# V products of batch 0 in two steps, and a new order of all steps around them, in a fused attention and gMLP kernel

## The chip, the cores and the metric

The kernel runs on one core of one Trainium2 chip. The metric is device time in microseconds (us) of one execution; the given time is the median of three runs. TensorE is called PE, VectorE DVE, ScalarE ACT, GpSimd POOL; SP issues the transfers.

## What is computed

Sliding-window attention over 8 batches, 8 heads, 576 positions and head size 64 (a query sees itself and the 63 positions before it), then a gMLP block on its output. Cut to what matters:

```python
scores = scale * np.matmul(q, k.transpose(0, 1, 3, 2))
rel = pos[:, None] - pos[None, :]
scores = np.where((rel >= 0) & (rel < 64), scores, -1e9)
attn = softmax(scores)
x = np.matmul(attn, v)            # (8, 576, 512) with heads side by side
h = np.maximum(x @ w_in, 0.0)     # w_in: 512 x 1024
u, v = h[..., :512], h[..., 512:]
v_n = (v - mean(v)) / np.sqrt(var(v) + 1e-06)
v_s = np.einsum('ts,bsd->btd', w_spatial, v_n) + b_spatial[None, :, None]
out = (u * v_s) @ w_out           # float32
```

## The kernel before

The work is cut into some 1,100 named steps. Each names the engine that runs it, what it depends on and which buffers it takes. A list, ORDER, gives every step in the order of emission as `name:engine:buffer`. Each engine runs its own steps in that order, strictly one after the other, so the place of a step in the list sets what it waits behind. Where the engine is PH in place of PE, the step's matmuls of 128 output partitions are issued as two of 64 (`halves`, L588 to L593); steps with PE there issue them whole. The buffer number names a slot; a step that takes a slot waits until the last users of what was there are done.

In the names the first digit is the batch, and `_g` is a group of four heads, `_gu` a pair of heads (u is 0 or 1) of a group, r the last 64 positions.

- ldq, ldk, ldv: transfers on SP's queue (L404, L425), in slots "nat" (8) and "natv" (4). ldwin, ldwsp, ldwo and ldb bring the weights (L330, L346, L387, L355) through the same "nat" slots.
- cq, ck, cv: cast to 16 bits, on POOL (L299, L302, L304; q and k in three pieces), DVE (L304) or ACT (L296). sl, su, s4 shift v by 64 positions. cwin, cwsp, cwo cast weights, cb the bias row.
- tq, tk: transpose on DVE (L411). S: scores on PE (L471, L539 for r). E: exponential on ACT (L478, L549). M: mask by a minimum on DVE (L481, L553). Z: row sums on PE (L494, L562). N and n: logarithm and its negative exponential on ACT, the reciprocal (L521, L523). P: products with v on PE (L506, L575). X: the division on DVE, which writes one head pair of x (L514, L583).
- V: `x @ w_in[:, 512:]` for 128 positions, four accumulated products, one for each head pair r of x (L657 to L661). V_4 is for the last 64 positions and takes along the last 64 output rows of the batch before (L673, L676). Vr, Vb, Va: Relu on ACT (L640), statistics and aggregate on DVE (L642, L644). L1, L2: the inverse deviation on ACT (L687, L689). A: normalisation on DVE (L699).
- U and Ur: the other half of `x @ w_in`, and its Relu (L728). W and We: w_spatial transposed on PE (L371), and copied out. G: the spatial product over five A tiles (four and one with the bias row). Ge: its product with u on DVE (L758). O: the output product, Oe its copy (L617), st its transfer.
- D: 27 matmuls on zeros (L798) that keep PE busy while the first data is on its way: 25 of two 512-column products, D25 and D26 of nine 128-column ones.

W_k needs all five cwsp casts, G needs all A steps of its batch and all We. Before V0 can begin there must be x of batch 0 and the casts of the second half of w_in.

## Time and profile before

| | us |
|---|---|
| median of three runs | 199.06 (198.86 to 200.04) |
| the profiled execution | 197.47 |
| its span, first to last instruction | 195.7 |
| PE / DVE / ACT / POOL busy in it | 186.3 / 164.1 / 150.0 / 111.3 |
| granted PE clock, mean | 0.998 |

How the rows of the profile are read. A row of the timeline has start, duration, engine, line of the kernel, operation, output<-input, shapes, and the count of instructions merged; in brackets the idle time of the engine before it and what ended that. A row of waits has who waited for whom, the total, how often, and the longest. A row of a stretch has its length and then each engine's busy time with its count of instructions, in the order PE, PE's weight loads, DVE, ACT, POOL, then the granted clock, the share of time in which the 16 DMA engines were busy, and GB/s. Ends of matmuls are modelled: consecutive rows of PE overlap by up to 0.2 us, and the start of the next row tells more than the duration.

### The profile page before, as it was taken

Reading aid. Unit: us, or ns where it says so; the run is one execution under the profiler, and the core shown is the slowest. Engines: PE = TensorE matmul, PEld = TensorE weight load, DVE = VectorE, ACT = ScalarE, POOL = GpSimd, SP = SyncE. Lnnn points to the kernel's source line nnn. Section 1 sums busy time; section 2 is a strip of 40 time slices with the busy share of each in tenths; the row PEclk is TensorE's granted clock in tenths of the full one; section 3 lists DMA queues with packets and bytes.
Section 4 is the critical chain, followed back from the end, with each engine's and each line's share of the span. In section 5 each row is a group of like instructions: output and inputs, shape, how many; then the busy total and the mean of one; then the engine's idle time right before and its main releaser. Section 6 shows DMA issues by size and latency. Waiting matters only on the chain.

```text
span 195.7 us, 7663 instructions
## 1 busy us (share of the span) xinstructions
PE 186.3 (95%) x3230; PEld 106.8 (55%) x3230; DVE 164.1 (84%) x305; ACT 150.0 (77%) x281; POOL 111.3 (57%) x196
## 2 busy tenths in 40 slices
...
GB/s 210 378 302 183 364 372 225 297 343 384 241 246 301 352 170 275 315 208 300 289 258 220 290 166 180 280 134 51 293 132 155 66 0 113 150 0 2 180 116 191
DMA packets 50277, 42.73 MB, mean 218 GB/s; under 512 B 39361, under 2 KB 39489, under 8 KB 50242
## 3 DMA queue, kind: packets, MB, share of 16 engines
...
q8 instruction: 25, 0.41, 0.9%
q10 hardware_dynamic: 224, 0.33, 0.5%
...
## 4 chain that ended last, share of the span: by engine, by line
PE 61%; DVE 14%; DMA 8%; SPq 6%; POOL 5%; issue 2%; ACT 2%; POOLq 0%; DVEq 0%
PE bank L593 38%; PE bank L590 10%; SPq L425 5%; DMA nv<-in_v_dram 3%; PE pair L471 3%; DVE e L481 3%; PE bank L506 3%; DVE kT L411 3%; DMA wi<-in_moe_w_in_dram 3%; DMA nk<-in_k_dram 3%; PE bank L673 3%; DVE vn L699 2%; PE bank L494 2%; POOL hk L299 2%; DVE x L514 1%
## 5 line engine op out<-in xcount | busy, mean ns | idle before, releaser
L478 ACT ACTIVATE e<-pair 128x1024 f16<-128x1024 f32 x32 | 31.5, 1025 | 13.5 <-PE pair L471 13.0
L593 PE MATMUL bank<-wspT,vn 128*64 128x512 f16 (+3 forms) x490 | 35.6, 290 | 0.6 <-DVE vn L699 0.4
L299 POOL CAST hk<-nk 128x384 f16<-128x384 f32 x42 | 22.5, 569 | 17.7 <-DMA nk<-in_k_dram 9.6
L758 DVE TENSOR_TENSOR g<-bank,ru 128x512 f16<-128x512 f32 (+1 forms) x40 | 24.5, 625 | 7.5 <-PE bank L593 4.5
L642 DVE BATCH_NORM_STATS2 st<-vs 128x6 f32<-128x512 f16 (+1 forms) x40 | 26.1, 669 | 4.6 <-ACT vs L640 4.4
L640 ACT ACTIVATE vs<-bank 128x512 f16<-128x512 f32 (+1 forms) x40 | 23.2, 595 | 8.6 <-PE bank L593 6.3
L302 POOL COPY hs<-hv 64x512 f16<-64x512 f16 (+1 forms) x46 | 28.4, 644 | 1.2
L617 ACT COPY ob<-bank 128x512 f32<-128x512 f32 (+1 forms) x39 | 22.1, 589 | 8.4 <-PE bank L590 6.4
L593 PE MATMUL bank<-x,win 128*64 128x512 f16 (+1 forms) x328 | 27.6, 308 | 0.0
L593 PE MATMUL bank<-win,x 128*64 128x512 f16 x208 | 26.2, 380 | 0.2 <-DVE x L514 0.2
L481 DVE TENSOR_TENSOR e<-e,mask 128x1024 f16<-128x1024 f16 x32 | 25.1, 803 | 0.8 <-ACT e L478 0.7
L299 POOL CAST hq<-nq 128x384 f16<-128x384 f32 x39 | 21.3, 583 | 5.9 <-DMA nq<-in_q_dram 3.6
L593 PEld LDWEIGHTS <-vn 128*64 128x64 f16 (+1 forms) x490 | 18.1, 111 | 11.8 <-DVE vn L699 1.4
L728 ACT ACTIVATE ru<-bank 128x512 f32<-128x512 f32 (+1 forms) x40 | 21.6, 555 | 3.3 <-PE bank L593 3.1
L593 PE MATMUL bank<-wout,g 128*64 128x512 f16 x184 | 22.6, 379 | 0.0
L514 DVE TENSOR_TENSOR x<-bank,lz 128x512 f16<-128x512 f32 x32 | 21.0, 681 | 1.4 <-PE bank L506 1.2
L411 DVE STREAM_TRANSPOSE kT<-hk 128x576 f32<-128x576 f32 x16 | 19.9, 1243 | 1.2 <-POOL hk L299 1.2
L521 ACT ACTIVATE lz<-bank 128x512 f32<-128x512 f32 x32 | 18.8, 598 | 2.6 <-PE bank L494 2.5
L699 DVE TENSOR_SCALAR vn<-vs,mv,ln 128x512 f16<-128x512 f16 (+1 forms) x40 | 17.3, 482 | 3.9 <-ACT ln L689 3.9
L302 POOL CAST hv<-nv 128x512 f16<-128x512 f32 x24 | 17.1, 738 | 5.4 <-DMA nv<-in_v_dram 5.0
L523 ACT ACTIVATE lz<-lz 128x512 f32<-128x512 f32 x32 | 19.8, 636 | 0.3
L411 DVE STREAM_TRANSPOSE qT<-hq 128x576 f32<-128x576 f32 x16 | 19.8, 1240 | 0.1
...
## 6 DMA issues: line engine op xcount, KB each, us to landing
...
ws<-in_moe_w_spatial_dram SPq DMA_DIRECT2D x4, 288.0 KB, 6.7
...
```

The lines of the kernel that those rows point to most:

```text
L299: nc.gpsimd.tensor_copy(o[:, n:n + 384], i[:, n:n + 384])
L302: nc.gpsimd.tensor_copy(o[:, lo:hi, :, :], i[:, lo:hi, :, :])
L411: d = add(f"t{name}{b}_{g}", ("DVE", 1.09), key, lambda e: nc.vector.transpose(qt.t[:, :].rearrange("p (i j) -> p j i", j=18), h.t[:, :].b ...
L478: ex = add(f"E{b}_{g}{u}", ("ACT", 0.91), key, lambda e, u=u: nc.scalar.activation(e2[u].t[:, :, :], sc[u].t[:, :, :], AF.Exp, bias=0.0, s ...
L481: mins.append(add(f"M{b}_{g}{u}", ("DVE", 0.65), key, lambda e, u=u: nc.vector.tensor_tensor(e2[u].t[:, :, :], e2[u].t[:, :, :], mask[:, : ...
L514: lambda e, u=u, ob=ob, lz=lz: nc.vector.tensor_tensor(x.t[:, u, :], ob.t[:, :], lz.t[:, :], ALU.mult),
L593: nc.tensor.matmul(o[c:c + 64, :], w[:, c:c + 64], x, start=start, stop=stop)
L617: lambda e: (nc.vector.tensor_copy if last else nc.scalar.copy)(view(), m.t[rows, 0:n]),
L640: rl = add(f"Vr{b}_{j}", ("ACT", 0.49), key, lambda e: nc.scalar.activation(vs.t[0:jn, :], m.t[0:jn, :], AF.Relu), deps=[pv], acq=[vs], us ...
L642: s1 = add(f"Vb{b}_{j}", ("DVE", 0.6), key + 0.02, lambda e: nc.vector.bn_stats(st6.t[0:jn, 0:6], vs.t[0:jn, :]), deps=[rl], acq=[st6], us ...
L728: lambda e, m=m, ru=ru, n=n: nc.scalar.activation(ru.t[:, 0:n], m.t[:, 0:n], AF.Relu), deps=[pu], acq=[ru], uses=[m])))
L758: lambda e, m=m, g=g, ru=ru, n=n: nc.vector.tensor_tensor(g.t[:, 0:n], m.t[:, 0:n], ru.t[:, 0:n], ALU.mult),
```

## The change

Three things change.

1. The four V steps of batch 0 over 128 positions (V0_0 to V0_3) are cut in two. Y0_j makes the products of head pairs 0 and 1 (group 0), V0_j then those of pairs 2 and 3 (group 1) into the same bank. Y0_j depends on X0_00 and X0_01 and two of the w_in casts alone. Y0_2, Y0_3 and V0_3 run ahead of Z1_00, the others later.
2. ORDER is another list. The transfers keep their order but for ldwin101, which goes ahead of ldwin110 and ldwin111; some take other slots. 32 steps have another engine, 25 of them in the first third of the list: ck0_0 (DVE to POOL), ck0_1 (POOL to ACT), cq1_0 (DVE to ACT), cv0_10, cwin111 and cwin010 (DVE to POOL), cwin011 (ACT to POOL), cwin100 and cwsp2 (POOL to DVE), su0_10 and s40_1 (ACT to DVE), su0_00 and s40_0 (POOL to ACT), We0 and We2 (DVE to ACT), We4 (ACT to DVE), sl1_00 (DVE to POOL), su1_01, cv1_11, sl1_11 and cq2_0 (ACT to POOL), cv1_10, sl1_10, su1_10 and ck2_1 (POOL to ACT). After them cwo01 goes to ACT and cwo10 to POOL, s44_1, s45_0 and su6_00 from ACT to POOL, cv7_10 and sl7_10 from POOL to ACT.
3. 114 steps stand as PH where 109 did: 16 names are new among them (Y0_0 is one), 11 are gone.

No arithmetic is added or removed: the matmuls of Y0_j and V0_j together are those of V0_j before. The diff, with the list cut to its start (to S3_0, the first scores of batch 3) and its end (from V7_4):

```diff
-D10:PE:0 D23:PE:1 D20:PE:2 D24:PE:3 D4:PE:0 D13:PE:1 D5:PE:2 ldq0_0:DQ:0 cq0_0:DVE:0 D15:PE:3
-tq0_0:DVE:0 D6:PE:0 ldk0_0:DQ:1 ldk0_1:DQ:2 ck0_1:POOL:1 ldq0_1:DQ:3 ldv0_00:DQ:0 D3:PE:1
-ldq1_0:DQ:4 ck0_0:DVE:2 tk0_0:DVE:1 D16:PE:2 tk0_1:DVE:2 D26:PE:3 S0_0:PE:0:1 E0_00:ACT:0
-ldk1_0:DQ:5 ldv0_10:DQ:1 ldv0_11:DQ M0_00:DVE cq0_1:POOL:3 tq0_1:DVE:3 D14:PE:0 D17:PE:1 D19:PE:2
-E0_01:ACT:1 D21:PE:3 S0_1:PE:0:1 M0_01:DVE E0_10:ACT:2 E0_11:ACT:3 ldv0_01:DQ ldv0_02:DQ Z0_01:PE:0
-N0_01:ACT:0 D7:PE:1 cq1_0:DVE:0 ck1_0:POOL:2 D25:PE:2 tq1_0:DVE:4 cv0_10:DVE:0 sl0_10:POOL:0
-su0_10:ACT D0:PE:3 D1:PE:1 cv0_00:POOL:1 M0_10:DVE S0_r:PE:0:1 E0_r0:ACT:0 E0_r1:ACT Z0_00:PE:2
-ldv0_12:DQ ldv0_03:DQ ldwin100:DQ:6 ldv0_04:DQ M0_11:DVE tk1_0:DVE:5 sl0_00:POOL:1 su0_00:POOL
-M0_r:DVE Z0_10:PE:3 ldv0_13:DQ ldv0_14:DQ cv0_01:DVE Z0_11:PE:1 su0_01:DVE sl0_01:DVE cv0_11:DVE
-cwin100:POOL su0_11:DVE D11:PE:0 s40_0:POOL ldwin110:DQ:7 ldwin111:DQ ldwin101:DQ D18:PE:0 ldb:DQ:0
-ldk1_1:DQ:1 sl0_11:DVE N0_00:ACT:1 cwin101:POOL n0_01:ACT ldq1_1:DQ:2 D9:PE:2 D22:PE:0 N0_11:ACT:2
-n0_11:ACT n0_00:ACT cwin110:POOL D12:PE:2 ck1_1:POOL:1 P0_00:PE:1 cq1_1:POOL:3 ldwin000:DQ:3
-cwin000:POOL ldwin001:DQ ldwin010:DQ:4 D8:PE:0 N0_10:ACT:3 s40_1:ACT Z0_r:PE:2 N0_r:ACT:4 n0_10:ACT
-P0_01:PE:3 S1_0:PE:0:1 X0_00:DVE:0 X0_01:DVE P0_11:PE:0 cwin111:DVE P0_10:PE:1 D2:PE:2 X0_10:DVE:1
-ldwin011:DQ ldwsp3:DQ:5 ldwsp2:DQ:6 X0_11:DVE E1_01:ACT:0 M1_01:DVE E1_00:ACT:1 n0_r:ACT P0_r:PE:3
-V0_2:PH:2 X0_r:DVE:0 Vr0_2:ACT:0 V0_0:PE:1 Vr0_0:ACT:1 ldwsp1:DQ:7 ldwsp4:DQ:1 Vb0_2:DVE:0
-Z1_01:PE:0 M1_00:DVE N1_01:ACT:5 n1_01:ACT Vb0_0:DVE:1 V0_4:PE:3 Vr0_4:ACT:2 ldv1_00:DQ:2
-ldwsp0:DQ:2 ldv1_01:DQ Z1_00:PE:2 Va0_2:DVE tk1_1:DVE:0 V0_3:PE:1 tq1_1:DVE:1 N1_00:ACT:1
-cwin010:DVE ldv1_02:DQ cwsp3:POOL ldv1_03:DQ ldv1_04:DQ cb:POOL cwin001:ACT Vb0_4:DVE:2 Vr0_3:ACT:3
-Vb0_3:DVE:3 Va0_4:DVE V0_1:PE:0 Vr0_1:ACT:4 Vb0_1:DVE:4 Va0_1:DVE ldk2_0:DQ:3 ldv1_10:DQ:3
-ldv1_11:DQ ldq2_0:DQ:5 ldv1_12:DQ S1_1:PE:1:0 cwin011:ACT U0_1:PE:3 E1_10:ACT:3 Va0_0:DVE
-E1_11:ACT:2 Va0_3:DVE Ur0_1:ACT:0 U0_2:PE:2 M1_10:DVE M1_11:DVE ldv1_13:DQ ldv1_14:DQ U0_4:PE:1
-cwsp2:POOL L10:ACT:0 L20:ACT U0_0:PE:0 S1_r:PE:1:0 Ur0_4:ACT:1 ldk2_1:DQ:4 ldwo10:DQ:0 ldq2_1:DQ:6
-cwsp1:POOL A0_4:DVE Ur0_2:ACT:2 cwsp0:DVE Z1_11:PE:3 ldwo00:DQ:7 ldwo11:DQ A0_0:DVE:0 Ur0_0:ACT:3
-Z1_10:PE:1 A0_1:DVE:1 N1_10:ACT:0 cwsp4:POOL A0_3:DVE:2 W1:PE:2 We1:DVE ldwo01:DQ ldq3_0:DQ:1
-N1_11:ACT:3 E1_r0:ACT:1 E1_r1:ACT W0:PE:0 We0:DVE A0_2:DVE:3 ldv2_00:DQ:0 ldk3_0:DQ:2 ldv2_01:DQ
-cv1_00:POOL:2 sl1_00:DVE:2 W4:PE:1 We4:ACT W3:PE:3 su1_00:POOL ldv2_02:DQ ldv2_03:DQ ldv2_10:DQ:1
-ldv2_11:DQ W2:PE:2 s41_0:ACT We3:DVE U0_3:PE:0 We2:DVE G0_2:PH:1 cv1_01:POOL sl1_01:ACT ck2_0:POOL:0
-ldv2_12:DQ ldk3_1:DQ:3 ldv2_13:DQ ldv2_14:DQ ldv2_04:DQ M1_r:DVE su1_01:ACT ldv3_10:DQ:2
-cv1_10:POOL:3 sl1_10:POOL:3 su1_10:POOL n1_00:ACT s41_1:POOL Ur0_3:ACT:4 cq2_0:ACT:2 tk2_0:DVE:2
-cv1_11:ACT sl1_11:ACT su1_11:POOL P1_00:PE:3 X1_00:DVE:2 Ge0_2:DVE:0 G0_1:PH:2 Ge0_1:DVE:1
-ldq3_1:DQ:5 tq2_0:DVE:3 P1_01:PE:0 X1_01:DVE G0_3:PH:3 ck2_1:POOL:1 G0_0:PH:1 n1_11:ACT cq2_1:POOL:3
-P1_10:PE:2 ldv3_11:DQ Ge0_3:DVE:2 n1_10:ACT S2_0:PE:1:0 E2_00:ACT:1 X1_10:DVE:3 P1_11:PE:0 X1_11:DVE
-G0_4:PE:3 Ge0_4:DVE:3 M2_00:DVE tk2_1:DVE:0 E2_01:ACT:0 ldv3_12:DQ V1_3:PE:2 Vr1_3:ACT:5 Z1_r:PE:0
-cwo01:POOL ldq4_0:DQ:4 ldv3_13:DQ tq2_1:DVE:1 U1_1:PH:3 N1_r:ACT:2 n1_r:ACT Ur1_1:ACT:5 Ge0_0:DVE:4
-V1_0:PH:2 cwo10:ACT Z2_00:PE:0 N2_00:ACT:4 Vr1_0:ACT:6 M2_01:DVE V1_1:PH:3 Vr1_1:ACT:7 S2_1:PE:1:0
-P1_r:PE:0 X1_r:DVE:1 U1_2:PH:1 E2_11:ACT:3 Vb1_1:DVE:5 cwo11:POOL E2_10:ACT:2 Vb1_0:DVE:0 V1_2:PH:2
-Vr1_2:ACT:2 M2_11:DVE U1_0:PH:3 Ur1_2:ACT:2 cwo00:POOL Z2_01:PE:0 N2_01:ACT:1 M2_10:DVE cq3_0:POOL:0
-Vb1_3:DVE:2 tq3_0:DVE:4 Ur1_0:ACT:0 V1_4:PE:2 Vr1_4:ACT:1 U1_4:PH:1 ck3_0:POOL:2 Ur1_4:ACT:4
-Vb1_4:DVE:4 S2_r:PE:0:1 Va1_0:DVE Z2_10:PE:0 N2_10:ACT:5 E2_r0:ACT:0 E2_r1:ACT Vb1_2:DVE:1 Va1_2:DVE
-Va1_3:DVE n2_01:ACT Va1_4:DVE Oe0_4:ACT:0 Va1_1:DVE L11:ACT:1 L21:ACT M2_r:DVE tk3_0:DVE:5
-A1_2:DVE:4 A1_0:DVE:5 U1_3:PH:3 O0_0:PH:1 Oe0_0:ACT:0 O0_1:PH:0 Oe0_1:ACT A1_3:DVE:6 cv2_00:POOL:1
-O0_2:PH:2 S3_0:PE:0:1 Oe0_2:ACT:1 Z2_11:PE:1 ldv5_10:DQ:3 Ur1_3:ACT:1 sl2_00:POOL:0 Z2_r:PE:0
...
-U7_1:PH:2 Vb7_1:DVE:4 Ur7_3:ACT:2 Ur7_1:ACT:3 V7_4:PE:1 Va7_2:DVE Oe6_2:ACT:1 U7_4:PE:0 O6_1:PE:2
-O6_3:PE:3 Va7_1:DVE Vr7_4:ACT:5 Oe6_4:ACT:0 Vb7_4:DVE:0 Va7_4:DVE O6_0:PE:1 Va7_3:DVE Va7_0:DVE
-L17:ACT:1 Ur7_4:ACT:4 L27:ACT A7_4:DVE U7_2:PE:0 A7_2:DVE:4 A7_3:DVE:5 Oe6_0:ACT:0 Oe6_1:ACT
-U7_0:PE:1 st6_0:DQ st6_4:DQ A7_1:DVE:6 Oe6_3:ACT A7_0:DVE:7 G7_1:PE:2 Ur7_2:ACT:5 G7_0:PE:3
-Ur7_0:ACT:1 Ge7_0:DVE:5 Ge7_1:DVE:6 G7_2:PE:0 Ge7_2:DVE:7 G7_3:PE:1 Ge7_3:DVE:8 G7_4:PE:3 st6_1:DQ
-Ge7_4:DVE:9 O7_2:PE:2 Oe7_2:ACT:0 st7_2:DQ O7_0:PE:0 Oe7_0:ACT:1 st7_0:DQ O7_1:PE:1 Oe7_1:ACT
+ldq0_0:DQ:0 D18:PE:0 D14:PE:1 D22:PE:2 D17:PE:3 D20:PE:0 ldk0_0:DQ:1 ck0_0:POOL:0 D15:PE:1 D4:PE:2
+ldk0_1:DQ:2 D6:PE:3 ldq0_1:DQ:3 ldv0_00:DQ:0 D7:PE:0 cq0_1:POOL:1 D13:PE:1 cq0_0:DVE:2 tq0_0:DVE:0
+ck0_1:ACT:3 ldq1_0:DQ:4 ldk1_0:DQ:5 ck1_0:POOL:2 D1:PE:2 ldv0_10:DQ:1 ldv0_11:DQ ldv0_01:DQ
+tk0_0:DVE:1 D3:PE:3 tk0_1:DVE:2 D23:PE:0 tq0_1:DVE:3 D11:PE:1 cv0_00:POOL:0 ldv0_02:DQ S0_0:PE:0:1
+E0_01:ACT:0 D5:PE:2 cv0_10:POOL:1 D26:PE:3 ldv0_12:DQ ldv0_03:DQ ldwin100:DQ:6 E0_00:ACT:1 M0_00:DVE
+S0_1:PE:1:0 Z0_00:PE:0 sl0_10:POOL:0 cq1_0:ACT:0 tq1_0:DVE:4 E0_10:ACT:2 D2:PE:1 D16:PE:2 D12:PE:3
+E0_11:ACT:3 ldv0_04:DQ ldv0_13:DQ D25:PE:1 sl0_00:POOL:1 ldv0_14:DQ ldwin101:DQ ldwin110:DQ:7
+cwin101:POOL D9:PE:2 D24:PE:3 cwin110:POOL M0_01:DVE N0_00:ACT:0 n0_00:ACT su0_00:ACT tk1_0:DVE:5
+ldwin111:DQ ldb:DQ:0 S0_r:PE:1:0 D10:PE:1 ldk1_1:DQ:1 ldq1_1:DQ:2 M0_10:DVE Z0_10:PE:0 Z0_01:PE:2
+cb:POOL M0_11:DVE E0_r0:ACT:0 E0_r1:ACT ldwin000:DQ:3 ldwin001:DQ ldwin010:DQ:4 ldwin011:DQ
+cv0_01:DVE D19:PE:3 cwin111:POOL M0_r:DVE ck1_1:POOL:3 ldwsp3:DQ:5 ldwsp2:DQ:0 su0_10:DVE
+cq1_1:POOL:1 ldwsp1:DQ:7 ldwsp4:DQ:1 ldv1_00:DQ:2 Z0_11:PE:1 N0_11:ACT:1 N0_01:ACT:2 sl0_01:DVE
+s40_0:ACT ldwsp0:DQ:2 ldv1_01:DQ ldv1_02:DQ Z0_r:PE:3 D0:PE:1 N0_10:ACT:3 cwin100:DVE D8:PE:2
+cv0_11:DVE sl0_11:DVE S1_0:PE:1:0 su0_01:DVE P0_01:PE:1 n0_10:ACT P0_00:PE:2 su0_11:DVE cwin000:POOL
+cwin010:POOL cwin011:POOL n0_01:ACT s40_1:DVE P0_10:PE:0 n0_11:ACT X0_00:DVE:0 cwsp3:POOL X0_01:DVE
+X0_10:DVE:1 P0_11:PE:2 X0_11:DVE N0_r:ACT:4 ldv1_03:DQ D21:PE:3 P0_r:PE:1 cwsp4:POOL ldv1_04:DQ
+n0_r:ACT ldk2_0:DQ:6 E1_00:ACT:0 M1_00:DVE Y0_2:PE:3 E1_01:ACT:1 Y0_3:PE:0 V0_3:PE X0_r:DVE:0
+Vr0_3:ACT:0 M1_01:DVE Z1_00:PE:2 V0_4:PE:1 N1_00:ACT:5 Vr0_4:ACT:1 Z1_01:PE:0 ldv1_10:DQ:3
+Vb0_3:DVE:0 Va0_3:DVE tk1_1:DVE:0 tq1_1:DVE:1 ldv1_11:DQ n1_00:ACT ldq2_0:DQ:4 Vb0_4:DVE:1 Y0_0:PH:2
+V0_0:PE cwin001:ACT V0_2:PE Vr0_0:ACT:2 Vr0_2:ACT:3 Y0_1:PE:1 ldv1_12:DQ N1_01:ACT:0 V0_1:PH
+Vr0_1:ACT:4 ldv1_13:DQ ldv1_14:DQ ldk2_1:DQ:3 Vb0_2:DVE:2 n1_01:ACT cwsp2:DVE S1_1:PE:1:0
+E1_11:ACT:2 Vb0_1:DVE:3 Vb0_0:DVE:4 U0_1:PH:2 ldwo10:DQ:5 E1_10:ACT:3 Ur0_1:ACT:0 U0_2:PH:3
+U0_4:PE:0 Ur0_4:ACT:1 Ur0_2:ACT:2 U0_0:PH:1 S1_r:PE:0:1 M1_10:DVE cwsp0:DVE Va0_4:DVE cwsp1:POOL
+cv1_00:POOL:2 sl1_00:POOL:2 ldq2_1:DQ:0 Va0_0:DVE Va0_1:DVE E1_r0:ACT:1 W3:PE:2 Va0_2:DVE L10:ACT:0
+L20:ACT M1_11:DVE We3:DVE A0_4:DVE A0_0:DVE:0 ldwo00:DQ:1 ldwo11:DQ ldwo01:DQ su1_00:POOL
+ldq3_0:DQ:7 ldv2_00:DQ:0 A0_2:DVE:1 cv1_01:POOL ldk3_0:DQ:2 ldv2_01:DQ ldv2_02:DQ W0:PE:0 W4:PE:3
+W1:PE:2 We4:DVE Ur0_0:ACT:3 We0:ACT W2:PE:1 E1_r1:ACT M1_r:DVE We1:DVE A0_1:DVE:2 U0_3:PE:0
+A0_3:DVE:3 We2:ACT Z1_11:PE:3 ck2_0:POOL:0 s41_0:ACT Z1_10:PE:1 N1_10:ACT:2 G0_3:PH:2 tk2_0:DVE:2
+Ur0_3:ACT:4 Ge0_3:DVE:0 ldv2_03:DQ ldv2_10:DQ:1 sl1_01:ACT N1_11:ACT:3 n1_10:ACT su1_01:POOL
+cq2_0:POOL:2 cv1_10:ACT:3 ldv2_11:DQ ldv2_12:DQ cv1_11:POOL ldk3_1:DQ:6 ldv2_13:DQ ldv2_14:DQ
+G0_4:PE:1 Ge0_4:DVE:1 tq2_0:DVE:3 G0_1:PE:0 Ge0_1:DVE:2 sl1_10:ACT:3 s41_1:POOL P1_00:PE:2
+X1_00:DVE:2 P1_01:PE:1 X1_01:DVE su1_11:POOL ldv2_04:DQ ldv3_10:DQ:2 ldq3_1:DQ:4 ldv3_11:DQ
+G0_2:PH:3 sl1_11:POOL Ge0_2:DVE:3 ldv3_12:DQ S2_0:PE:0:1 su1_10:ACT P1_11:PE:0 P1_10:PE:2
+cq2_1:POOL:3 X1_10:DVE:3 ldq4_0:DQ:0 n1_11:ACT X1_11:DVE E2_01:ACT:0 E2_00:ACT:1 ck2_1:ACT:1
+M2_00:DVE cwo11:POOL G0_0:PH:1 Z1_r:PE:3 N1_r:ACT:1 n1_r:ACT Ge0_0:DVE:4 U1_0:PH:2 Ur1_0:ACT:5
+V1_3:PH:0 tk2_1:DVE:0 Z2_00:PE:3 N2_00:ACT:4 Vr1_3:ACT:5 V1_2:PH:1 Vr1_2:ACT:6 M2_01:DVE V1_0:PH:2
+Vr1_0:ACT:7 n2_00:ACT tq2_1:DVE:1 cwo00:POOL cq3_0:POOL:0 Vb1_3:DVE:5 V1_1:PH:3 Vr1_1:ACT:1
+Vb1_1:DVE:0 Va1_1:DVE P1_r:PE:0 X1_r:DVE:1 U1_1:PH:1 Vb1_0:DVE:1 cwo10:POOL cwo01:ACT S2_1:PE:1:0
+Ur1_1:ACT:4 E2_11:ACT:2 E2_10:ACT:3 tq3_0:DVE:4 Vb1_2:DVE:4 U1_2:PH:2 Ur1_2:ACT:1 U1_4:PH:3
+Z2_01:PE:1 Ur1_4:ACT:0 N2_01:ACT:5 V1_4:PE:0 Vr1_4:ACT:2 Va1_3:DVE S2_r:PE:0:1 M2_11:DVE M2_10:DVE
+ldv3_13:DQ ldv5_10:DQ:3 E2_r0:ACT:0 Va1_0:DVE O0_2:PE:2 Va1_2:DVE O0_1:PE:3 U1_3:PE:1 ck3_0:POOL:2
+Oe0_2:ACT:0 Vb1_4:DVE:3 Va1_4:DVE tk3_0:DVE:5 E2_r1:ACT Oe0_4:ACT:0 O0_0:PE:2 cv2_00:POOL:0
+sl2_00:POOL:0 su2_00:POOL cv2_10:POOL:1 L11:ACT:1 L21:ACT n2_01:ACT S3_0:PE:0:1 O0_3:PH:0 M2_r:DVE
...
+Va7_3:DVE X7_r:DVE:1 V7_4:PE:3 Vr7_4:ACT:0 Vb7_4:DVE:4 U7_0:PH:2 Ur7_0:ACT:4 O6_3:PH:0 Oe6_4:ACT:0
+O6_2:PE:2 Va7_4:DVE Va7_1:DVE L17:ACT:1 L27:ACT A7_2:DVE:4 A7_0:DVE:5 A7_1:DVE:6 O6_1:PE:3
+A7_3:DVE:7 Oe6_0:ACT:0 A7_4:DVE Oe6_1:ACT G7_0:PE:1 Ge7_0:DVE:5 G7_3:PE:3 Ge7_3:DVE:6 st6_0:DQ
+Oe6_2:ACT:1 Oe6_3:ACT st6_4:DQ G7_1:PE:2 Ge7_1:DVE:7 U7_4:PE:0 G7_2:PE:1 Ge7_2:DVE:8 G7_4:PE:3
+st6_1:DQ O7_2:PE:2 Oe7_2:ACT:0 O7_0:PE:1 Ur7_4:ACT:5 O7_1:PE:2 O7_3:PE:0 st7_2:DQ Oe7_0:ACT:1
+Oe7_1:ACT st7_0:DQ st7_1:DQ Oe7_3:ACT st7_3:ACT Ge7_4:DVE:9 O7_4:PE:3 Oe7_4:DVE:0 st7_41:ACT
...
@@ -192,6 +193,9 @@
 
 
 CHOOSE = as_listed
+
+
+SPLIT = (0,)
 
 
 HALVED = {w.split(":")[0] for w in ORDER.split() if w.split(":")[1] == "PH"}
@@ -654,14 +658,20 @@
             m = buf("bank", f"pv{b}_{j}")
             vs = buf("vs", f"vs{b}_{j}")
 
-            def emit_V(e, j=j, m=m):
-                with nc.named_scope(f"V{b}_{j}"):
-                    for r in range(4):
-                        halves(f"V{b}_{j}", m.t, xr(b, r)[:, 128 * j:128 * j + 128],
+            def emit_V(e, name, rs, j=j, m=m):
+                with nc.named_scope(name):
+                    for r in rs:
+                        halves(name, m.t, xr(b, r)[:, 128 * j:128 * j + 128],
                                w_in_sb[r][:, 512:1024], r == 0, r == 3)
-            pv = add(f"V{b}_{j}", ("PE", 0.86), key + 0.1 + 0.03 * j, emit_V,
-                     deps=[XD[b, r] for r in range(4)] + [WIN[1, r] for r in range(4)],
-                     acq=[m], uses=[XB[b, 0], XB[b, 1]], mode="f")
+            pv = None
+            for name, rs in (("Y", (0, 1)), ("V", (2, 3))) if b in SPLIT else (("V", range(4)),):
+                name = f"{name}{b}_{j}"
+                pv = add(name, ("PE", 0.215 * len(rs)), key + 0.1 + 0.03 * j,
+                         lambda e, name=name, rs=rs, f=emit_V: f(e, name, rs),
+                         deps=[XD[b, r] for r in rs] + [WIN[1, r] for r in rs] + [pv],
+                         acq=[] if pv else [m],
+                         uses=[XB[b, r] for r in sorted({r // 2 for r in rs})] + ([m] if pv else []),
+                         mode="f")
             stat_steps(b, j, m, vs, pv, key + 0.1 + 0.03 * j, VS, ST)
         m = buf("bank", f"pv{b}_4")
         vs = buf("vs", f"vs{b}_4")
```

159 lines of the change are left out of this document (80 added, 79 removed).

## The prediction

> **What bounds the kernel now.** I read the page first, then the waits of TensorE, then busy time by stretches, then the timelines of the engines over the first 60 us. All times are us from the span's start.
>
> ```profile
> PE 186.3 (95%) x3230; PEld 106.8 (55%) x3230; DVE 164.1 (84%) x305; ACT 150.0 (77%) x281; POOL 111.3 (57%) x196
> ```
>
> ```profile
> PE pair L471 <- DVE qT L411: 1.9, 2, 1.2
> ...
> PE bank L593 <- DVE vn L699: 0.4, 1, 0.4
> PE bank L593 <- DVE g L758: 0.2, 1, 0.2
> ```
>
> ```profile
> 30.00:60.00 30.00, 28.63 (x556) 17.07 (x557) 29.11 (x56) 28.14 (x54) 22.78 (x37) 1.00 1.06 290
> ```
>
> The first row says that TensorE fills 95% of the span. The next rows are its waits (total, times, longest). The first comes from the whole span and lies before 33 us. The last two are everything that TensorE waits for after 60 us: 0.6 us in 135. So from 60 us on the kernel is matmul work at a fixed rate, and no order can win more than 0.6 us there. The last row is the stretch 30 to 60 us (PE, PEld, DVE, ACT, POOL busy, clock, DMA share): DVE is busy 29.11 of 30 us and the DMA engines are full (1.06). Whatever the new order wins or loses without bound, it does in the first 60 us, where DVE and the transfers set the pace.
>
> **The split V step, and the way to S1_1.** The PE timeline around it:
>
> ```profile
> 24.14 0.96 PE L593 MATMUL bank<-win,x 128*64 128x512 f16 x6
> 25.29 0.41 PE L593 MATMUL bank<-win,x 128*64 128x512 f16 x2 [0.19 <-DVE x L514]
> ...
> 30.78 0.67 PE L471 MATMUL pair<-qT,kT 32*128 32x128 f16 x56 [0.67 <-DVE qT L411]
> ...
> 34.77 0.62 PE L494 MATMUL bank<-e,ones 128*64 128x512 f16 x4
> 35.34 2.40 PE L371 MATMUL bank<-id,wnat 128*128 128x128 f16 x25
> 37.68 1.04 PE L590 MATMUL bank<-x,win 128*128 128x512 f16 x4
> 38.64 1.27 PE L593 MATMUL bank<-wspT,vn 128*64 128x512 f16 x10
> ```
>
> The first two rows are V0_2: six of its eight half products run before the last head pair of x is there, and only the last two wait. So a V step already starts on the pairs it has; from 24.14 to 25.29+0.41 it takes 1.56, where an undisturbed step shows 1.03 (the row at 47.75 further down). The split can win at most 0.5 us. Behind it stands S1_1 (30.78), idle 0.67 for the transposed q of batch 1. What comes earlier in V0 only makes that wait longer; the split alone is worth nothing, and S1_1 moves only if DVE does.
>
> ```profile
> 6.84 0.74 DVE L304 CAST hk<-nk 128x1152 f16<-128x1152 f32 x1
> ...
> 13.68 1.05 DVE L304 CAST hq<-nq 128x1152 f16<-128x1152 f32 x1
> ...
> 15.87 0.41 DVE L304 CAST hv<-nv 128x512 f16<-128x512 f32 x1
> ...
> 23.25 0.79 DVE L304 CAST win<-wi 128x512 f16<-128x512 f32 x1
> ...
> 25.16 0.85 DVE L481 TENSOR_TENSOR e<-e,mask 128x1024 f16<-128x1024 f16 x1
> ...
> 27.74 0.68 DVE L642 BATCH_NORM_STATS2 st<-vs 128x6 f32<-128x512 f16 x1
> ...
> 29.49 1.23 DVE L411 STREAM_TRANSPOSE qT<-hq 128x576 f32<-128x576 f32 x1
> ```
>
> Ahead of X0_11 (which ends where M1_01 begins, 25.2) DVE loses the first four casts: 0.74+1.05+0.41+0.79 = 3.0. It is given su0_10, cwin100 and s40_1, at most about 0.6+0.8+0.4 = 1.8 by these same shapes. Against the 1.2 net stand new idle times: k of head group 0 is now cast by POOL, so DVE waits where it worked, and fourteen plain warm-up steps stand ahead of S0_0 instead of eleven and a short one, so the first exponentials start some 0.8 later (three of half a V step, 0.43 each, less about 0.5). I take X0_11 at 25.2 as before (bounds: 1.2 earlier, 0.7 later). From there to the end of tq1_1 (29.49+1.23) the new queue has one statistics step less (0.68): S1_1 at 30.1 instead of 30.8.
>
> **The spatial weights pin it again.**
>
> ```profile
> 28.21 0.33 SPq L346 DMA_DIRECT2D ws<-in_moe_w_spatial_dram  x1
> ```
>
> ```profile
> ws<-in_moe_w_spatial_dram SPq DMA_DIRECT2D x4, 288.0 KB, 6.7
> ```
>
> ```profile
> 32.85 0.31 DVE L644 BATCH_NORM_AGGREGATE mv<-st 128x2 f32<-128x6 f32 x3
> ...
> 34.84 0.44 DVE L304 CAST wnat<-ws 128x576 f16<-128x576 f32 x1
> 35.21 1.04 DVE L699 TENSOR_SCALAR vn<-vs,mv,ln 128x512 f16<-128x512 f16 x3
> ...
> 36.92 0.64 DVE L699 TENSOR_SCALAR vn<-vs,mv,ln 128x512 f16<-128x512 f16 x1
> ...
> 38.93 0.42 DVE L553 TENSOR_TENSOR er<-er,maskr 128x512 f16<-128x512 f16 x1
> ...
> 42.64 1.24 DVE L411 STREAM_TRANSPOSE qT<-hq 128x576 f32<-128x576 f32 x1
> ...
> 44.97 1.29 DVE L514 TENSOR_TENSOR x<-bank,lz 128x512 f16<-128x512 f32 x2
> ```
>
> The last spatial block, ldwsp0, is issued at 28.21 (it needs the buffer of q1_1, whose cast keeps its place on POOL); with 6.7 to landing it is there at about 34.9, and its cast at 34.84 shows the same. The transfers keep their order and their engines are full, so this doesn't move. The five W steps need that cast, so they start at 35.3 in both kernels, and the 0.7 won at S1_1 becomes idle time in front of W3. Worse, before, Z1_11 and Z1_10 (34.77, 0.57 to the next step, of which 0.1 is a change of tile shape, below) filled that place; now they stand behind U0_3. G0's first step comes at 35.3 + 2.34 (W) + 0.96 (U0_3) + 0.45 = 39.05 instead of 38.64.
>
> There the normalised V must be ready. Before, three of its aggregates (32.85) and M1_11 lie ahead of cwsp0, and the last of its A steps ends at 36.92+0.64 = 37.56. Now ACT puts N1_01, Vr0_1 and n1_01 ahead of batch 1's exponentials, so M1_10 comes late, and DVE's queue has behind cwsp0 four aggregates (0.4), M1_11 (0.8, as M1_01), three We (0.4 each, as the cast of the same size at 34.84), five A (0.35 each, 35.21) and M1_r (0.4): 4.55 us, to 39.8. The fourth product of G0_3 needs the last A step and is due at 39.05 + 3 x 0.22 = 39.7, so it waits 0.1. PE is 0.5 later here for the same work.
>
> Next, q of batch 2 moves from ACT to POOL:
>
> ```profile
> 41.16 1.15 ACT L296 CAST hq<-nq 128x1152 f16<-128x1152 f32 x1 [0.65 <-DMA nq<-in_q_dram]
> ```
>
> ```profile
> 9.72 1.41 POOL L299 CAST hq<-nq 128x384 f16<-128x384 f32 x3
> 13.34 2.21 POOL L299 CAST hk<-nk 128x384 f16<-128x384 f32 x3 [2.21 <-DVE qT L411]
> ...
> 26.32 1.86 POOL L299 CAST hq<-nq 128x384 f16<-128x384 f32 x3
> ```
>
> The data lands at 41.16, so ACT ended at 42.31; POOL ends between 42.6 (1.41) and 43.4 (2.21). I take 43.0, by the third row, since DVE is as busy there. tq2_0 then runs at 43.0, not 42.64, and S2_0 on PE waits for it. Behind it DVE now has six steps of 0.64 (44.97, two in 1.29) up to X1_11, which ends at 48.1, where before it ended at 46.26. U1_0, the first product of batch 1, needs X1_11 and ends at about 48.3; before, the same amount of PE work was done one step of 0.86 ahead of 47.75, at 46.9: 1.4 later.
>
> Some of it comes back. Before, batch 2's second score step ran from 49.79 to 51.02 (next fence), 1.23 for the 0.67 that S1_1 took, and DVE is too far behind now for this 0.56 to be lost again. I put PE at S3_0 (the row at 59.68) 0.9 later, between 0.3 and 1.4.
>
> **Halves and the end.**
>
> ```profile
> 47.75 1.03 PE L593 MATMUL bank<-win,x 128*64 128x512 f16 x8
> 48.61 0.38 PE L494 MATMUL bank<-e,ones 128*64 128x512 f16 x2
> 48.83 1.03 PE L593 MATMUL bank<-win,x 128*64 128x512 f16 x8
> 49.79 0.54 PE L471 MATMUL pair<-qT,kT 32*128 32x128 f16 x40
> ...
> 50.72 0.30 PE L471 MATMUL pair<-qT,kT 32*128 32x64 f16 x16 [0.40 <-issue]
> ...
> 59.68 0.67 PE L471 MATMUL pair<-qT,kT 32*128 32x128 f16 x56 [0.21 <-DVE kT L411]
> ```
>
> ```profile
> 176.89 0.38 PE L673 MATMUL bank<-win,x 128*64 128x512 f16 x1
> ...
> 180.59 1.70 DVE L699 TENSOR_SCALAR vn<-vs,mv,ln 64x512 f16<-64x512 f16 x5 [0.87 <-ACT ln L689]
> ```
>
> A halved step takes 0.86 (47.75 to 48.61). In front of a score step it takes 0.96 (48.83 to 49.79), and a whole one in front of a halved one the same (37.68 to 38.64). So a whole and a halved step cost alike, and each change of tile shape costs 0.1. Counted in the two lists behind S1_1, changes between 64- and 128-column steps go from 6 to 8, changes into score steps stay 19: +0.2.
>
> At the end V7_4 starts at 176.89 and the last of the five A7 steps ends at 180.59+1.70 = 182.29: 5.4 us. The new list has V7_4, U7_0, three O6 steps and the first four products of G7_0 in between, 5 x 0.86 + 0.1 + 0.87 = 5.3, and one Relu more on ACT in the chain: 0.2 lost, between 0 and 0.5. Moves among ACT and POOL behind 60 us (s44_1, s45_0, su6_00 to POOL; cv7_10, sl7_10 to ACT) lie beside PE work; without that cover they cost 0.4 to 1.0 each. The waits of 0.6 behind 60 us I leave as they are.
>
> Sum: 0.9 + 0.2 + 0.2 = 1.3 us. On the profiled execution (197.47, of which the span is 195.7) that gives 198.8; the runs' median is 199.06, 1.6 above it, and on that I forecast **200.4 us**. Own range 199.2 to 201.8.
>
> [...] The DVE cast with POOL idle took 0.74 (6.84), the one beside POOL's cast 1.05 (13.68), and POOL's took 2.21 instead of 1.41: both pay, neither stops wholly. [...]
>
> **Rivals.**
> 1. *The early gain is kept* (chance 0.14). If the landing of ldwsp0 moves with the rest, or POOL's cast of q2_0 takes 1.41, then DVE's 2 to 3 us of removed casts count. W3 then starts up to 0.7 earlier, and the waits of 0.5 at S2_1 and up to 0.6 behind 60 us go: 199.06 - 0.7 - 0.5 - 0.3 + 0.4 = 198.0, at best 197.2. For it: DVE was busy 29.11 of 30 us. Against it: the row at 34.84.
> 2. *POOL becomes what the scores wait for* (0.24). In the first 50 us POOL is given cv0_10, three w_in casts, sl1_00, su1_01, q2_0, cv1_11 and cwo10 against nine others, some 1.3 us net by the shapes. If each q or k cast there takes 2.21 (the row at 13.34) and DVE's steps stretch from 0.74 to 1.05 beside them, cq2_0 ends at 43.4, and with 1.3 us more ahead of ck3_0 the transposes of batches 2 and 3 come 1.5 later still: 200.4 + 1.5 = 201.9. It decides once X1_11 ends after 48.8. [...] For it: a cast there did take 2.21. Against it: POOL is idle for 7 of these 30 us (22.78 busy), which can absorb it.
> 3. *The split does what it is said to do* (0.02 beside the first): V0 ends 0.5 earlier and S1_1 with it, 198.5 for the whole. The row at 30.78 speaks against it.
>
> The forecast has 0.60. A measurement of this kernel tells about 1% (2 us) from no change: 197.1 and 201.1 are the bounds. Faster: a fifth of the first rival, and little else, 0.04. Slower: 0.9 of the second and a fifth of the forecast, 0.33. Within 1%: 0.63. For 8 in 10 the range takes most of both rivals: 198.2 to 202.6.
>
> **What would show it.** Right: S1_1 at about 30 with W3 still at 35.2 to 35.4 and TensorE idle before it; the last A0 step at 39.5 or later; tq2_0 waiting for POOL at 43; X1_11 near 48; S3_0 0.5 to 1.3 after 59.7; a wait of some tenths inside G7_0. Wrong: W3 before 34.8, which makes the first rival likely, or waits of TensorE behind 60 us of well over 0.6 us, which this working can't place.

## The result and the profile after

The changed kernel takes 201.68 us (median of 4 runs, 201.07 to 202.22), the kernel before, beside it, 198.96 (4 runs, 198.11 to 200.04). The ratio is 1.0121, 95% interval 1.0073 to 1.0168: 2.4 us slower (1.5 to 3.3), where 1.3 were forecast. Ratios, and the median of e9 below, leave out executions over 1.5% above a kernel's fastest. The direction and both ranges held, the author's own (199.2 to 201.8) by 0.1; the sum was too small. The time lies above the prediction's bound of 201.1 for "within 1%", so what it gave 0.33 came true, not what it gave 0.63.

The profiled execution of the changed kernel took 201.81, with a span of 200.1. First the busy times on its page, then the stretch that was shown of before:

```profile
PE 189.1 (95%) x3258; PEld 107.4 (54%) x3258; DVE 164.1 (82%) x302; ACT 153.0 (76%) x282; POOL 107.3 (54%) x197
```

```profile
30.00:60.00 30.00, 28.72 (x509) 16.43 (x509) 27.57 (x50) 26.09 (x50) 23.19 (x39) 0.94 1.04 279
```

In this stretch DVE, which was busy 29.11 of 30 us, is now busy 27.57. It has no less to do on the way to batch 3: from tq1_1 to tk3_0, both counted, its busy time is 29.2 us before and 30.2 now. It waits. The clock column says 0.94. TensorE's and VectorE's timelines at the places that the prediction named (start, duration, ..., idle before and what ended it):

```profile
29.97 0.67 PE L475 MATMUL pair<-qT,kT 32*128 32x128 f16 x56
...
35.36 2.40 PE L375 MATMUL bank<-id,wnat 128*128 128x128 f16 x25 [1.09 <-DVE wnat L308]
37.69 1.88 PE L594 MATMUL bank<-x,win 128*128 128x512 f16 x4
...
61.36 0.67 PE L475 MATMUL pair<-qT,kT 32*128 32x128 f16 x56 [0.42 <-DVE kT L415]
```

```profile
31.51 0.46 DVE L308 CAST wnat<-ws 128x576 f16<-128x576 f32 x1 [0.54 <-DMA ws<-in_moe_w_spatial_dram]
...
34.39 0.92 DVE L308 CAST wnat<-ws 128x576 f16<-128x576 f32 x1
...
39.62 1.01 DVE L709 TENSOR_SCALAR vn<-vs,mv,ln 128x512 f16<-128x512 f16 x2
...
44.05 1.26 DVE L415 STREAM_TRANSPOSE qT<-hq 128x576 f32<-128x576 f32 x1 [0.88 <-POOL hq L303]
```

S1_1 starts at 29.97, W3 at 35.36 after 1.09 idle, both as forecast. The last A0 step ends at 40.63, tq2_0 waits to 44.05, and S3_0 comes at 61.36 instead of 59.68. S3_0 waits for tk3_0 on DVE; the idle rows of DVE ahead of it are what to look at. The place of S3_0 flatters the new list a little: the row sums Z2_10 and the mask M2_r, 0.22 and 0.4 us by their likes, stand ahead of it in the old list and behind it in the new one.

The kernel before was profiled a second time in the experiments (b_again, one execution, 199.72, span 198.0). The first profile, on which the prediction stands, took 197.47 and was among its quickest executions. TensorE's waits behind 60 us in that second profile, and in the changed kernel:

```profile
PE bank L593 <- DVE vn L699: 1.1, 2, 0.8
PE pair L471 <- DVE qT L411: 0.8, 1, 0.8
```

```profile
PE bank L597 <- DVE x L518: 0.7, 1, 0.7
PE pair L475 <- DVE kT L415: 0.4, 1, 0.4
PE bank L566 <- DVE er L557: 0.2, 1, 0.2
PE bank L597 <- DVE vn L709: 0.2, 1, 0.2
PE bank L597 <- ACT vs L644: 0.2, 1, 0.2
```

The 0.6 us of waits that the prediction took for the kernel's own were 1.9 in another execution of the same kernel. The changed kernel's 1.7, of which 0.4 is S3_0's own wait, are not more than that, so single profiles can't price the part behind 60 us.

The place of S1_1 moves from one execution to the next as well. Its rows with the old list, in b_again and in e2 (below):

```profile
30.19 0.67 PE L471 MATMUL pair<-qT,kT 32*128 32x128 f16 x56 [0.67 <-DVE qT L411]
29.38 0.67 PE L474 MATMUL pair<-qT,kT 32*128 32x128 f16 x56 [0.67 <-DVE qT L414]
```

In the four profiles with the old list and no split (before, b_again, e2, e6) S1_1 comes at 29.38 to 30.78, in the nine that begin with the new list at 29.26 to 30.54, by the means at 30.0 and 29.9. The first profile, with 30.78, was the latest of them all, so a gain of 0.7 at S1_1 is not shown.

### The profile page after: what moved, and what is told of

Its sections match the earlier page's. It is cut to its first block, busy times and chain, and to the rows that moved or that the text cites. A ratio compares the mean times of both kernels' runs of the same rounds, so it can differ in the third digit from the quotient of the medians.

```text
span 200.1 us, 7710 instructions
## 1 busy us (share of the span) xinstructions
PE 189.1 (95%) x3258; PEld 107.4 (54%) x3258; DVE 164.1 (82%) x302; ACT 153.0 (76%) x282; POOL 107.3 (54%) x197
## 4 chain that ended last, share of the span: by engine, by line
PE 63%; DVE 14%; ACT 9%; DMA 7%; issue 3%; POOL 2%; POOLq 0%; ACTq 0%
PE bank L597 39%; PE bank L594 8%; PE bank L808 5%; DMA nq<-in_q_dram 4%; DMA ws<-in_moe_w_spatial_dram 3%; PE bank L510 3%; PE pair L475 3%; DVE e L485 2%; DVE qT L415 2%; DVE x L518 2%; ACT e L482 2%; DVE vn L709 2%; PE bank L498 2%; PE bank L683 2%; DVE g L768 1%
## 5 line engine op out<-in xcount | busy, mean ns | idle before, releaser
L597 PE MATMUL bank<-wspT,vn 128*64 128x512 f16 (+3 forms) x490 | 36.3, 292 | 1.3 <-DVE x L518 0.7
L597 PE MATMUL bank<-x,win 128*64 128x512 f16 (+1 forms) x384 | 31.8, 304 | 0.1
L303 POOL CAST hq<-nq 128x384 f16<-128x384 f32 x42 | 21.9, 557 | 18.6 <-DMA nq<-in_q_dram 12.9
L306 POOL COPY hs<-hv 64x512 f16<-64x512 f16 (+1 forms) x46 | 26.6, 604 | 3.3 <-ACT hv L300 2.1
L303 POOL CAST hk<-nk 128x384 f16<-128x384 f32 x39 | 19.7, 539 | 14.6 <-DMA nk<-in_k_dram 8.2
L485 DVE TENSOR_TENSOR e<-e,mask 128x1024 f16<-128x1024 f16 x32 | 24.6, 784 | 0.9 <-ACT e L482 0.8
L597 PE MATMUL bank<-wout,g 128*64 128x512 f16 x184 | 23.3, 380 | 0.0
L709 DVE TENSOR_SCALAR vn<-vs,mv,ln 128x512 f16<-128x512 f16 (+1 forms) x40 | 19.3, 535 | 2.2 <-ACT ln L699 2.2
L597 PEld LDWEIGHTS <-win 128*64 128x64 f16 x384 | 15.7, 111 | 9.8 <-issue 0.4
```

The source lines that it names most:

```text
L303: nc.gpsimd.tensor_copy(o[:, n:n + 384], i[:, n:n + 384])
L306: nc.gpsimd.tensor_copy(o[:, lo:hi, :, :], i[:, lo:hi, :, :])
L485: mins.append(add(f"M{b}_{g}{u}", ("DVE", 0.65), key, lambda e, u=u: nc.vector.tensor_tensor(e2[u].t[:, :, :], e2[u].t[:, :, :], mask[:, : ...
L597: nc.tensor.matmul(o[c:c + 64, :], w[:, c:c + 64], x, start=start, stop=stop)
L709: ENG[e].tensor_scalar(o[0:jn, :], VS[j].t[0:jn, :], mv_t[b % NSB][0:jn, j, 0:1], ln.t[0:jn, 5 + j:6 + j], ALU.subtract, ALU.mult)
```

## The experiments

Ratios are to the kernel before, run beside each. "Old" and "new" are the two lists; where they are joined, a few steps take other buffer slots. Line numbers in the profiles shift by a few where the list is longer or shorter.

Two joined lists share out the loss. **e1: the new list to S3_0, then the old**:

```diff
 (new list)  ... D10:PE:0 ... S3_0
+(old list, what is left)  ... O7_3
```

> The new list up to S3_0 (first scores of batch 3), behind it the steps that are left in the order of the kernel before. Theory A, the prediction's: the loss is made ahead of S3_0, by DVE's queue around the spatial weights and by the cast of q of batch 2. The trace of the changed kernel has S3_0 1.7 us later (61.36 against 59.68) and no loss can come behind it here: 200.6 us. Rival B: the loss is made behind S3_0, where from there to O7_3 the new list took 133.0 us and the old one 130.5: 199.3 us here. Both at once would show as a part of the 2.7 us in each of this run and the next.

Measured: 202.77, ratio 1.0211 (1.0167 to 1.0254).

**e2: the old list to S3_0, without the split, then the new**:

```diff
-SPLIT = (0,)
+SPLIT = ()
 (old list)  ... S3_0
+(new list, what is left)  ... O7_3
```

> The old list up to S3_0, without the split V steps, behind it the new list. Theory A: 199.3 us, the 0.4 that the prediction gave to changes of tile shape and to the end. Rival B: 201.3 us, the 2.3 us net that the trace shows behind S3_0; TensorE then waits for x and the normalised V near the P4 and G3 steps as in the changed kernel.

Measured: 200.09, ratio 1.0060 (1.0033 to 1.0086), so the new order behind S3_0 costs 1.2 us. e1 costs 4.2, more than the whole change: where the lists meet, TensorE waits 1.7 us for logarithms of row sums, so its time is no price of the first part. Its start of S3_0 is: 61.14.

**e3: cq2_0 on ACT again**, all else as changed; **e4: two filler steps on zeros ahead of W3**, four matmuls more, so that TensorE isn't idle there:

```diff
-cq2_0:POOL:2
+cq2_0:ACT:2
```

```diff
+D27:PE:0 D28:PE:0
 W3:PE:2
```

> The changed kernel with the cast of q of batch 2, head group 0, on ACT as before instead of POOL, at the same place of the list. Theory A as predicted: the cast ends 1.15 instead of 1.40 to 1.55 behind its landing, tq2_0 and S2_0 come 0.3 to 0.4 earlier and so does all behind them: 201.3 us. Rival: S2_0 is set by the landing (42.46 in the changed kernel, 41.16 at the latest before) or what is won is lost behind S3_0: 201.7 us. If POOL's cast were the main cost, DVE's idle 0.88 ahead of tq2_0 would go: 200.8 us.

> The changed kernel with two more filler steps (two 512-column products each, 0.86 us in all) between S1_r and W3, where TensorE stands idle for 1.1 us; behind that gap the granted clock falls to 0.77 in 35 to 40 us, and U0_3 takes 1.81 instead of 0.96. Theory C, the clock costs the time: it stays at 1.0, G0_3 starts at 39.1 instead of 40.4, and the kernel takes 200.3 us. Theory D, the slow stretch is hidden, since A0_3 ends at 40.6 and tq2_0 at 45.3 whatever TensorE does: the clock stays at 1.0 and the time at 201.7 us. If the idle time isn't what lowers the clock, it falls again and nothing changes.

Measured: 202.38 (ratio 1.0168, 1.0128 to 1.0208) and 202.12 (1.0147, 1.0104 to 1.0191). Neither wins anything. The stretches 35 to 40 and 40 to 45 us of the changed kernel, then of e3 and of e4 (the last three columns are clock, DMA share, GB/s):

```profile
35.00:40.00 5.00, 4.64 (x33) 2.29 (x35) 5.00 (x15) 2.85 (x7) 4.76 (x8) 0.77 1.04 306
40.00:45.00 5.00, 5.00 (x75) 2.66 (x73) 3.81 (x6) 4.30 (x8) 2.82 (x6) 0.89 1.06 346
```

```profile
35.00:40.00 5.00, 4.10 (x35) 2.39 (x35) 5.00 (x14) 3.00 (x9) 4.69 (x8) 1.00 1.02 304
40.00:45.00 5.00, 4.84 (x73) 2.36 (x73) 3.90 (x7) 4.91 (x9) 3.21 (x6) 1.00 1.08 331
```

```profile
35.00:40.00 5.00, 4.56 (x36) 2.39 (x35) 4.78 (x14) 2.85 (x7) 3.23 (x6) 1.00 0.99 274
40.00:45.00 5.00, 4.86 (x73) 2.36 (x72) 4.12 (x7) 4.86 (x9) 4.35 (x9) 1.00 1.07 309
```

In the changed kernel the granted clock falls to 0.77 and 0.89 here, in the two others it stays at 1.00, and S3_0 comes at 61.20 and 60.97, 0.2 and 0.4 earlier: the slower clock lies beside VectorE's wait and costs little there, and nothing that the medians show. VectorE's own row in e3:

```profile
43.79 1.25 DVE L415 STREAM_TRANSPOSE qT<-hq 128x576 f32<-128x576 f32 x1 [1.10 <-ACT hq L300]
```

With ACT as the caster the wait is still there, 1.10 instead of 0.88: the data was there at 41.28, but ACT gets to it at 42.62, behind its reciprocals. So taking the cast off POOL doesn't take the wait away; what a caster that is free at once would win, e3 doesn't show.

**e5: the split alone in the old list; e6: the new list's marks of whole and halved steps alone** (26 steps); **e7: the new list to S1_1, then the old**:

```diff
-V0_2:PH:2 ... V0_0:PE:1
+Y0_2:PH:2 Y0_0:PE:1 V0_2:PH ... V0_0:PE
-V0_3:PE:1 ... V0_1:PE:0
+Y0_3:PE:1 V0_3:PE ... Y0_1:PE:0 V0_1:PE
```

```diff
-U0_1:PE:3 ... G0_1:PH:2 ... O0_0:PH:1 ... U2_4:PE:0 ... O6_3:PE:3
+U0_1:PH:3 ... G0_1:PE:2 ... O0_0:PE:1 ... U2_4:PH:0 ... O6_3:PH:3
```

```diff
 (new list)  ... S1_1
+(old list, what is left)  U0_1 ... O7_3
```

> The old order of steps with the split alone: Y0_2 and Y0_0 ahead of the first half of each V product of batch 0, Y0_3 and Y0_1 directly ahead of the second. Theory A (the split is worth nothing by itself, since the product already began on the pairs it had and S1_1 still waits for tq1_1): 199.0, S1_1 at 30.6 to 30.9. Rival (the split does what it says, TensorE starts earlier and keeps it): 198.4, S1_1 by 30.2 or S3_0 half a microsecond earlier than 59.7.

> The old order of steps, no split, but each gMLP step whole or in halves as the new list has it (26 steps differ). Theory A (a step takes the same time whole or halved, what changes is the number of changes of tile shape): 199.2, two or three tenths over the kernel before. Rival (the marks are most of the late loss, since halves bring VectorE and ScalarE more, shorter instructions and free the banks otherwise): 199.8 or more, with waits of TensorE behind 60 us of 1 or more. A third: no difference at all, 199.0; then the late loss is one of order alone.

> The new order with the split up to S1_1, the old order of the remaining steps from there. Theory A (what S1_1 wins is lost again at the first W step, which waits for the spatial weights; the loss of 1.5 is made between S1_1 and S3_0, in the queue of VectorE and GpSimd behind the new order of Z1, A0 and cq2_0): 199.0, W at 35.2 to 35.6, X1_11 at 46 to 46.5, S3_0 at 59.4 to 59.8. Rival 1 (the gain at S1_1 is kept): 198.2, S3_0 at 59.0. Rival 2 (the loss comes from ahead of S1_1, by the order of the transfers and casts there): over 200, S3_0 at 60.5 or later.

Measured: e5 199.46, ratio 1.0021 (0.9988 to 1.0055). The split alone is worth nothing that can be measured (0.2 us won to 1.1 lost), S1_1 is at 30.41.

e6: 200.65, ratio 1.0087 (1.0054 to 1.0120), 1.7 us, where theory A's 199.2 was too low by a miscount. In the old order these marks leave 58 priced changes of tile shape (all but those out of a score step) where there were 39. At the prediction's 0.1 each that is 1.9. The rows of the second profile of before, then of e6, for the same pair of steps, O6_2 and its successor:

```profile
177.44 1.03 PE L593 MATMUL bank<-wout,g 128*64 128x512 f16 x8
178.30 1.03 PE L593 MATMUL bank<-x,win 128*64 128x512 f16 x8
```

```profile
177.85 1.04 PE L590 MATMUL bank<-wout,g 128*128 128x512 f16 x4
178.81 1.05 PE L593 MATMUL bank<-x,win 128*64 128x512 f16 x8
```

From start to start 0.86 becomes 0.96, because a whole step (128*128) now stands among halved ones (128*64). The rival's sign, waits behind 60 us of 1 or more, is there too (1.2), but b_again has 1.9 without these marks. Without waits of over 0.15 us TensorE takes 133.6 from S3_0 to its last matmul in e6, 131.3 and 131.9 in the two profiles of before: the loss lies in its own rows, though not each change was priced apart. The new list itself has 42 such changes, so they explain 0.3 of its loss.

e7: 202.56, ratio 1.0172 (1.0134 to 1.0210), S3_0 at 63.18. Theory A is wrong; time and S3_0 are rival 2's. S1_1 itself is early (29.37), so the loss isn't there yet. TensorE's row behind it:

```profile
35.81 1.06 PE L497 MATMUL bank<-e,ones 128*64 128x512 f16 x4 [2.38 <-DVE e L484]
```

TensorE waits 2.38 for M1_11 on DVE. DVE had waited 1.1 at cwsp2 for the transfer (the new list has this cast on DVE, the old on POOL), and its M1_10 and M1_11 then took 2.2 beside POOL's casts, 1.5 and 2.1 in the two profiles of before. So the time goes at the spatial weights, on DVE, by a cast that stands ahead of S1_1 in the list: in this, rival 2 is right.

**b_again: before, unchanged, for a second profile.**

> The kernel before once more, for a second profile of it: the first profiled execution took 197.47, below the median of its own runs. Theory: 199.0, the places of S1_1, W, X1_11 and S3_0 within 0.4 of the first profile, and the 1.5 by which 199.0 exceeds 197.47 spread over the span or ahead of the first load. Rival: an execution of 199 shows a wait of its own in one place.

It took 199.72. S1_1, W, X1_11 and S3_0 lie within 0.6 of the first profile; of the 2.3 us by which its span is longer, 2.0 lie behind S3_0, 1.3 of them in the waits shown above. That is nearer to the rival than to the theory, which had the difference spread or ahead of the first load and the places within 0.4.

VectorE's idle time from tq1_1 to tk3_0, added up from its records, sorts the profiles: 0.74 to 1.23 with the old list up to S3_0 (before 0.89, b_again 0.74, e6 0.87, e2 1.23; e5, with the split, 1.58), 2.09 to 3.49 with the new one (changed 2.43, e1 2.09, e3 3.49, e4 2.90). Its busy time doesn't: 29.1 to 30.4 in all of these. S3_0 comes at 59.39 to 59.96 in before, b_again, e6 and e2, and at 60.97 to 61.36 in the four with the new list: 1.5 later by the means (59.70 and 61.17). The profile of e5 is between them: its load of q of batch 2 landed late, S3_0 came at 61.01, and what followed was quick.

In the changed kernel this idle time stands ahead of cwsp2 (0.54), M1_10 (0.16), Ge0_3 (0.32), tq2_0 (0.88) and Vb1_1 (0.47); in e1 none of it is at tq2_0.

The last four kernels try to take that idle time away, and one late wait. **e8: cwsp2 on POOL, the Va0 steps and M1_11 earlier; e9: X4_00 ahead of two A3 steps; e10: both, and tq2_0 behind Ge0_1 and X1_00**:

```diff
+cwsp2:POOL
 cwsp4:POOL
...
-cwsp2:DVE
...
-M1_10:DVE cwsp0:DVE Va0_4:DVE ... Va0_0:DVE Va0_1:DVE ... Va0_2:DVE ... M1_11:DVE
+Va0_4:DVE Va0_0:DVE Va0_1:DVE Va0_2:DVE M1_11:DVE M1_10:DVE cwsp0:DVE
```

```diff
-A3_4:DVE A3_0:DVE:4 A3_1:DVE:5 A3_3:DVE:6 ... A3_2:DVE:7 ... X4_00:DVE:0
+A3_4:DVE A3_0:DVE:4 A3_3:DVE:6 ... X4_00:DVE:0 A3_1:DVE:5 A3_2:DVE:7
```

```diff
-tq2_0:DVE:3 ... Ge0_1:DVE:2 ... X1_00:DVE:2
+Ge0_1:DVE:2 ... X1_00:DVE:2 tq2_0:DVE:3
```

> The changed kernel with cwsp2 on GpSimd again, ahead of cwsp4 there, and on VectorE Va0_4, Va0_0, Va0_1, Va0_2 and M1_11 ahead of M1_10. Theory A (the early loss is idle time of VectorE, which was full before: it waits at cwsp2 for a transfer, and M1_11 and A0 stand behind casts that wait): its idle time from tq1_1 to tk3_0 falls from 2.4 to 1.7 or less, M1_11 ends before 34.4, the last A0 by 39.9, S3_0 at 60.4 or earlier, 200.8. Rival (the transfer of q of head pair 0 of batch 2 sets the pace, whatever stands ahead of it): the idle time turns up ahead of tq2_0, 1.5 or more there, tq2_0 ends at 45.0 or later, S3_0 at 61.0 to 61.4, 201.7.

> The changed kernel with A3_1 and A3_2 behind X4_00 on VectorE instead of ahead of it. Theory A (a part of the late loss is the wait of G3_3 for the bank that X4_00 frees): Z4_r to G3_3 takes 0.2 instead of 1.0, nothing later gives it back, 200.9. Rival (the time is given back, G3_1 or G3_2 wait for A3_1 and A3_2, or a later wait grows by as much): 201.7.

> The two edits together, and tq2_0 behind Ge0_1 and X1_00 on VectorE, so that it has work while q of batch 2 is still under way. Theory A (early and late loss are VectorE's order and add up): idle time of VectorE from tq1_1 to tk3_0 at 1.3 or less, S3_0 at 60 or earlier, 200.0, half of what the change lost won back or more. Rival (S2_0, which now comes 0.7 later, costs as much as VectorE wins): S3_0 at 61 or later, 201 and more.

Measured: e8 201.66 (ratio 1.0138, 1.0099 to 1.0177), e9 201.2 (1.0124, 1.0087 to 1.0161), e10 201.85 (1.0143, 1.0106 to 1.0179). None wins against the changed kernel's 1.0121. S3_0 comes at 60.65 in e8, where theory A had 60.4, and at 60.93 in e10, where it had 60. VectorE's waits from 28 to 61 us, in e8 and in e10:

```profile
DVE wspT L308 <- PE bank L375: 1.1, 1, 1.1
DVE qT L415 <- POOL hq L303: 0.8, 1, 0.8
DVE wnat L308 <- DMA ws<-in_moe_w_spatial_dram: 0.7, 1, 0.7
```

```profile
DVE wspT L308 <- PE bank L375: 1.6, 1, 1.6
DVE qT L415 <- POOL hq L303: 0.6, 1, 0.6
DVE g L768 <- PE bank L594: 0.5, 1, 0.5
```

The wait at cwsp2 is gone and stands later, at cwsp0 and We3, behind the same weights: 3.14 and 3.30 us idle in all. (The wait for qT in e10 is that of tq1_1, ahead of the stretch that is added up; tq2_0 waits no more there.) M1_11 no longer was what A0 stood behind; We3 was. So the repair chosen in e8 was wrong, though the place was right. In e9 the late theory falls. By time alone the gain of 0.8 us that it promised is barely excluded (a ratio of 1.0081, where the interval starts at 1.0087); the rows say more. Here are those of DVE and PE in the changed kernel, then in e9:

```profile
104.04 2.91 DVE L709 TENSOR_SCALAR vn<-vs,mv,ln 64x512 f16<-64x512 f16 x5 [1.14 <-ACT ln L699]
106.87 1.26 DVE L518 TENSOR_TENSOR x<-bank,lz 128x512 f16<-128x512 f32 x2
```

```profile
107.59 0.62 PE L597 MATMUL bank<-wspT,vn 128*64 128x512 f16 x4 [0.74 <-DVE x L518]
```

```profile
105.59 0.69 DVE L518 TENSOR_TENSOR x<-bank,lz 128x512 f16<-128x512 f32 x1 [0.37 <-PE bank L510]
106.20 1.40 DVE L709 TENSOR_SCALAR vn<-vs,mv,ln 128x512 f16<-128x512 f16 x2
```

```profile
106.33 0.41 PE L597 MATMUL bank<-wspT,vn 128*64 128x512 f16 x2
106.98 0.41 PE L597 MATMUL bank<-wspT,vn 128*64 128x512 f16 x2 [0.24 <-DVE vn L709]
```

G3_3 needs all five A3 steps. With X4_00 ahead it starts 1.3 earlier and stops inside, for A3_1 and A3_2: together 0.92 over an undisturbed step, against 0.90 before G3_3 in the changed kernel. The releaser named in the first profile was only the last of two.

**e11: e8's edits, tq2_0 behind X1_00, and the work around the W steps put back where it covers the wait for the weights**:

```diff
-ldv1_10:DQ:3 ... ldv1_11:DQ ... ldq2_0:DQ:4
+ldq2_0:DQ:4 ldv1_10:DQ:3 ... ldv1_11:DQ
-W3:PE:2 ... We3:DVE A0_4:DVE A0_0:DVE:0 ... U0_3:PE:0 ... Z1_11:PE:3 ... Z1_10:PE:1
+L10:ACT:0 L20:ACT ... Z1_11:PE:3 Z1_10:PE:2 W3:PE:0 A0_4:DVE A0_0:DVE:0 We3:DVE ... N1_11:ACT:3 N1_10:ACT:2 ... U0_3:PE:3
```

> The changed kernel (without the edit at X4_00) with the early edits of the run before, and the work around the spatial weights put back to where it fills the wait for them: L10, L20 directly behind the Va0 steps, Z1_11 and Z1_10 with their two reciprocal logarithms ahead of W3, A0_4 and A0_0 ahead of We3 on VectorE, and the load of q of head pair 0 of batch 2 ahead of ldv1_10 in the queue. Theory A (what the change lost ahead of S3_0 is idle time of VectorE at the two places where transfers set the pace, the spatial weights and q of batch 2): idle from tq1_1 to tk3_0 at 1.6 or less, the last A0 by 39.6, S3_0 at 60.2 or earlier, 200.6: the early half is back and the late half of 1.2 stays. Rival 1 (the transfers set the pace whatever is put ahead of them): the idle time is found again ahead of tk2_0 or tq2_0, 2 or more in all, S3_0 at 60.7 to 61.3, 201.7. Rival 2 (S3_0 comes by 60.2 and the end does not): 201.5, the loss ahead of S3_0 is not what the time goes by.

Measured: 201.16, ratio 1.0096 (1.0061 to 1.0131). TensorE's and VectorE's rows there:

```profile
34.47 0.62 PE L497 MATMUL bank<-e,ones 128*64 128x512 f16 x4 [0.30 <-ACT ru L737]
35.42 2.40 PE L374 MATMUL bank<-id,wnat 128*128 128x128 f16 x25 [0.33 <-DVE wnat L307]
```

```profile
34.62 0.74 DVE L307 CAST wnat<-ws 128x576 f16<-128x576 f32 x1 [0.71 <-DMA ws<-in_moe_w_spatial_dram]
35.28 1.17 DVE L708 TENSOR_SCALAR vn<-vs,mv,ln 64x512 f16<-64x512 f16 x2
36.38 0.43 DVE L307 COPY wspT<-bank 128x576 f16<-128x576 f16 x1
```

W3 still starts at 35.42; but Z1_11, and A0_4 and A0_0 on DVE, now run beside the wait for the weights and for the first W step. The last A0 ends at 39.38 and S3_0 comes at 60.10, as theory A said: 1.1 of the mean loss of 1.5 ahead of it is back. Which of the edits did it isn't told apart: the load of q of batch 2, now earlier in the queue, also landed at 39.70, the earliest of all profiles. Of the idle time 2.26 us remain, more than its 1.6. The time lies between theory A's 200.6 and rival 2's 201.5, and its interval reaches from e2's ratio to above that of the change, so by time alone it is open how much of what is won at S3_0 is kept. No version here beats the kernel before.

## Why the prediction came out as it did

- **The split alone is worth nothing, S1_1 at 30.1, W pinned.** On the split it was right: e5 is 1.0021. S1_1 came at 29.97 and W3 at 35.36, but that S1_1 fits is luck: the working took 0.7 off one late profile, and over all profiles the lists don't differ there. In all the profiles that record its landing, ldwsp0 lands between 33.8 and 35.2, as far apart with the old list (33.8 to 35.1) as with the new (34.0 to 35.2); none of the orders brought it forward. The first rival needed W3 before 34.8, which no profile with the new list shows, and is out, though its other condition, POOL's cast of q2_0 at 1.41, was met.
- **The last A0 step at 39.8.** It ended at 40.63. The step that failed is the five A steps at 0.35: they took 3.19, not 1.75, and cwsp0 0.92, not 0.44, all but 0.2 of it beside busy POOL. The prediction's own rows had a DVE cast at 1.05 beside POOL's for 0.74 with POOL idle; here the five A steps took 1.44 more than was reckoned. But the change didn't bring that: with the old list the five took 3.28 in b_again, 3.00 in e2 and 3.31 in e6. The 0.35 was the price of one quick execution, in which they took 2.23.
- **tq2_0 at 43.0 through POOL's cast.** It came at 44.05. POOL's cast took 1.41 (42.61 to 44.01), the lower bound, not the 1.86 taken. The q data came late: 42.46 instead of 41.16. "This doesn't move" was said of the weights; this load does move: it lands at 39.94 to 41.14 in before, b_again, e2 and e6 (43.29 in e5), at 41.09 to 42.46 in the changed kernel, e1, e3 and e4, and at 39.70 in e11, which put it further ahead in the queue. Why it came later in the changed kernel was not tried.
- **S3_0 0.9 later (0.3 to 1.4).** The mechanism was right in the main: loads that land late, and VectorE waiting behind them. The size was off: 1.7 between the two first profiles, 1.5 by the means. VectorE idles 1.8 us more ahead of tk3_0 (means of the same four and four, 0.93 and 2.73); e7, e8 and e11 show that the W steps are one place of it. The wait for q of batch 2 is another in the changed kernel, e3 and e4, but not in e1. The second rival, POOL, just reached its mark (X1_11 at 48.81) and nearly its time (201.9), but not by its cause: POOL has no more work than before (busy 31.0 of the first 50 us, before 32.5, b_again 32.0), tk3_0 waits for no POOL, and e3, which takes the cast off it, wins nothing.
- **Tile shapes, 0.2.** Right in price as far as e6 goes: 1.7 for 19 more changes, 0.09 each (0.06 to 0.13) if they are all of it. The prediction's own count for the new list was small and so is its share.
- **The end, 0.2, and the waits behind 60 us "as they are".** Together with the shapes 0.4 was forecast behind S1_1; e2 measures 1.2 (0.7 to 1.7) behind S3_0. This is the other term that was mis-sized. The step that failed is that the rest behind 60 us was put at nothing: the moves were to lie beside TensorE's work and the waits, 0.6 us by one quick execution, to stay as they are. Its own sign of being wrong, waits of well over 0.6, was met. The 0.2 for the end isn't seen: from the start of V7_4 (181.75) to the end of the last A7 step (187.18) it is 5.4 as before, and G7_0 doesn't wait inside. Where the 1.2 is lost is not settled. Two waits recur with the new list behind S3_0 and stand in no profile with the old list there: the one ahead of G3_3 in the changed kernel, e2, e3 and e4 (0.4 to 0.8), which e9 could not undo, and one of row sums for a mask step in three of these (0.2 to 0.6, not in e3). But other waits change from one execution to the next by as much. All waits of over 0.15 us behind S3_0 are 1.5 by the means of these four and 1.1 in before, b_again, e5 and e7, so most of the 1.2 stands in no such wait.

With 1.5 for 0.9 and 1.2 for 0.4 the sum is 2.7; 2.4 was measured. The two parts come from different sources, places in profiles and medians of times, and need not add up. The clock's fall behind W wasn't foreseen; by e3 and e4 it cost nothing that can be measured.
